# Retention and a two-layer network on one core: q cast without its decay, the decay multiplied into the retention's result, and a new order of the work

## The chip, the cores and the metric

The kernel runs on one core of a Trainium2 chip. The metric is the device time of one execution in microseconds. Three runs of the kernel before gave 282.3, 279.86 and 279.4; their median is 279.86.

The engines are called PE (matmul), DVE (vector), ACT (scalar), POOL and SP. PE's weight loads have a row of their own, PEld. Work that PE writes lands in PSUM; DVE and ACT read it there.

## The reference

q, k and v are f32 of shape 8 x 8 x 576 x 64 (batch, heads, positions, head size). For each batch and head, with gamma = 1 - 2^(-5-head):

```python
scores = scale * np.matmul(q, k.transpose(0, 1, 3, 2))
Dmat = np.where(rel >= 0, gamma[:, None, None] ** rel[None, :, :], 0.0)   # rel = row - column
ret = scores * Dmat
attn = np.matmul(ret, v)
...
x = attn.transpose(0, 2, 1, 3).reshape(B * S, H * D)       # 4608 tokens x 512
h = x @ w_in                                               # 512 x 2048
out = np.maximum(0.01 * h, h) @ w_out                      # 2048 x 512, f32
```

The factor gamma^(row - column) is gamma^row from the side of q times gamma^(-column) from the side of v, so either can be multiplied in on its own.

## The kernel before

**Units and groups.** The tokens are cut into 36 units of 128 tokens; each is two chunks of 64 positions of one batch (a batch has nine chunks). Four units make a group of 512 tokens, nine groups in all. A unit u goes through these jobs, by the names that the order's table uses:

- `ld{u}.1`, `.0`, `.2`: load k, q and v (256 KB each, f32) into one of four tiles each. SP issues k and q from unit 12 on and for unit 0, POOL the rest, the weights and most stores (line 346; w_in is line 612, in four quarters `wi0` to `wi3` of 512 KB as f16).
- `ck`, `cq`, `cv`: to f16. k is only cast (line 371). q is multiplied by scale * gamma^row and v by gamma^(-row): on DVE in one product with a broadcast table (line 375), on ACT in eight narrow multiplies, one for each head (line 381). Rows are counted within a block of 256 positions, and `place(c)` says in which quarter of the block a chunk c lies.
- `tp` and `yt`, for units 0 to 7: q and k are turned by PE (line 411) and copied out of PSUM (line 418). From unit 8 on `tr` turns them by a transposing DMA that SP issues.
- `sa` (scores, line 445) and `sb` (what each chunk adds to the state, line 454): 64x64 matmuls into the PSUM tile `sc`. From unit 4 on `sa` is part of `ca`. `mk` masks the scores from PSUM on DVE (line 460).
- `st`: the running state in f32 on DVE (lines 485 to 491); the one at a block's end goes through a scratch tile `stmp` and is scaled by gamma^256. `sx` casts it to f16.
- `oa`, or `ow` and `ca` from unit 4 on: outputs, 64x64 matmuls into the PSUM tile `ot` (line 542). `ot` has two slots; unit u writes slot u % 2, so `ca{u+2}` waits for the copy of unit u.
- `x{u}`: copies the unit's output from PSUM into the f16 tile xT of its group (line 591), on ACT for 31 units and on DVE for 5.

**The network.** Groups 0 and 1 go through w_in plainly (jobs `h` on PE, line 640, and `l` on ACT, line 647). From group 2 on layer 1 (`a`, line 833), and for all groups layer 2 (`b`, line 911), is done in seven products for eight with sums of operands made on DVE (`xs`, `m`, `ws`, `wm`), seeds copied from PSUM to PSUM (`cA`), and partial results copied out (`u2`, `k5`).

**What sets the order.** The code declares jobs with what they must come after. A long string, ORDER, names all of them in the sequence in which they are issued; each engine runs its own in that sequence. A word such as `tp1.0@0` gives the accumulator bank, and `+13@3` puts 13 matmuls on idle data in (the filler, line 980). The table ENGINE says which of DVE and ACT runs a copy or cast.

Of the kernel before, what the change touches and what calls it, by code (L numbers as in the profile page):

```python
# [33 lines left out]
class Plan:  # L34
# [52 lines left out]
    for eng, names in {  # L87
        "DVE": """
            ck0 cq0 sx0.0 yt0.0 cq1 sx0.1 cv1 cq2 sx1.0 yt2.1 ck3 cq3 yt3.1 cv3 sx2.1 yt3.0 cq4 cv4 x3 ck5 cq5
            cv5 yt5.1 cq6 sx5 cv6 cq7 ck7 cv7 yt7.0 b0.cA cv8 ck10 sx8.0 cv9 cq9 cq11 cq12 cv10 b1.cA cv13 ck15  # L90
            cv14 cq14 cv15 cq15 sx13.1 sx14 cq16 cv16 cv17 cq17 cq18 a2.3.k5 sx17.0 cv18 sx18 cq19 a3.1.u2 x17
            cv20 ck21 cq21 sx19 a3.2.k5 cq22 cv22 sx20 ck23 cv23 cq23 x20 cv24 cq25 sx23 a4.2.cA cv25 a4.2.u2
            cq26 cq27 cv27 sx25 a5.0.u2 a5.0.k5 cq28 cq29 cv29 ck30 cq30 cv30 ck31 cv31 cq32 sx30 cq33 ck33
            a6.0.cA cv33 cv34 ck34 cq35 cq34 a6.2.cA b5.u2 cv35 a6.3.u2 x32 a7.0.cA x33 a7.0.k5 b5.21 a7.1.cA
            b6.11 b6.u2 a7.3.cA a7.3.u2 a8.0.k5 b7.k5 a8.2.u2 a8.2.k5 b7.21 a8.3.u2 b8.21
        """,
        "ACT": """
            cv0 yt0.1 x0 ck1 ck2 yt1.1 yt1.0 cv2 yt2.0 x1 sx1.1 sx2.0 x2 sx3.0 ck4 sx3.1 yt4.1 yt4.0 ck6 sx4.1
            x4 yt5.0 x5 yt6.0 yt6.1 sx6 yt7.1 sx7 x7 x6 ck8 b0.11 cq8 ck9 b0.u2 cq10 b0.k5 cv11 ck12 sx9 x8 ck11
            cv12 sx10 cq13 b0.21 x9 ck13 sx11 b1.11 sx12 x10 b1.u2 x11 ck14 a2.0.cA b1.k5 a2.0.u2 a2.0.k5 x12  # L100
            a2.1.cA a2.1.u2 x13 a2.1.k5 ck16 ck17 sx15 a2.2.cA a2.2.u2 b1.21 a2.2.k5 sx16 x14 a2.3.cA x15
            a2.3.u2 ck18 b2.cA a3.0.cA b2.11 a3.0.u2 a3.0.k5 a3.1.cA cv19 b2.u2 x16 a3.1.k5 ck19 b2.k5 a3.2.cA
            ck20 cq20 a3.2.u2 cv21 b2.21 ck22 x18 a3.3.cA a3.3.u2 a3.3.k5 x19 b3.cA a4.0.cA b3.11 sx21 ck24
            a4.0.u2 a4.0.k5 cq24 a4.1.cA a4.1.u2 sx22.1 a4.1.k5 x21 b3.u2 ck25 b3.k5 ck26 sx24 a4.2.k5 x22 cv26
            a4.3.cA x23 a4.3.u2 a4.3.k5 ck27 b3.21 a5.0.cA b4.cA ck28 cv28 sx26.0 b4.11 x24 ck29 a5.1.cA a5.1.u2
            a5.1.k5 x25 sx27 sx28 b4.u2 a5.2.cA x26 sx29 b4.k5 a5.2.u2 a5.2.k5 x27 a5.3.cA ck32 a5.3.u2 cv32
            a5.3.k5 cq31 b4.21 x28 x29 sx31.1 a6.0.u2 a6.0.k5 sx32 b5.cA a6.1.cA b5.11 a6.1.u2 x30 a6.1.k5 x31
            a6.2.u2 a6.2.k5 sx33 b5.k5 ck35 a6.3.cA a6.3.k5 sx34 sx35.0 a7.0.u2 b6.cA a7.1.u2 a7.1.k5 a7.2.cA
            a7.2.u2 b6.k5 a7.2.k5 x34 x35 a7.3.k5 a8.0.cA b6.21 a8.0.u2 b7.cA b7.11 a8.1.cA b7.u2 a8.1.k5
            a8.1.u2 a8.2.cA a8.3.cA a8.3.k5 b8.cA b8.u2 b8.k5 b8.11x so8.11x b8.11y  # L110
# [26 lines left out]
    ld15.1 m1.0.1 ow10 b0.11 ca11 m1.2.0 a2.0.p1.0@2 b1.11 so0.0 b1.p5.0@0 m1.1.1 a2.0.cA@1 cv13 x10 b1.p5.1 mk11
    sx12 ld17.2 b1.p6.1 m1.2.1 m1.3.0 ow11 b1.u2 sb13 ca12 m1.3.1 a2.0.p2.0 x11 b1.p7.0 tr13 ld15.0 a2.0.11 xs2.0
    cq14 b1.k5 ld16.0 a2.0.p5.0@2 st13.1 b1.p7.1 a2.0.k5 xs2.1 ld17.0 mk12 a2.0.p6.0 xs2.2 b1.p3.0 a2.0.u2 sx13.1
    ck15 ck14 ld16.1 xs2.3 a2.0.p7.0 a2.0.p3.0 a2.0.22 b1.p3.1 a2.0.12 l2.0.22 a2.0.p4.0 b1.22 l2.0.12 a2.1.p1.0@2  # L140
    cv14 a2.0.21 b1.p4.0 b1.12 ld18.2 a2.1.p5.0@1 cq15 sb14 a2.1.k5 ow12 ca13 tr14 a2.1.cA@0 b1.p4.1 st14.0 x12
# [910 lines left out]
```

## Time and profile before

| | us |
|---|---|
| runs | 279.4, 279.86, 282.3 |
| the profiled execution's own time | 279.54 |
| its span in the profile | 277.7 |
| PE busy | 268.1 |
| PE weight loads busy | 224.4 |
| DVE busy | 229.8 |
| ACT busy | 206.7 |
| POOL busy | 72.4 |
| DMA, mean rate over the span | 180 GB/s |

The profile is one execution, taken by the hardware profiler; its span is shorter than the execution's time, since the span ends with the last instruction that the profile shows. Matmuls are pipelined, so a busy PE is one with a matmul under way, and the mean duration of one (273 ns for 128x256) is longer than the step from one to the next (0.87 us for eight, 109 ns each, in the chain of work that ended last). That chain is PE for 91% of the span and DMA for 5%. In a group's row stand line, engine, operation, tiles, shapes and count, then busy time and mean ns of one, then the engine's idle time just before and what ended it.

### The profile page before, as it was taken

How to read it: one execution, taken by the hardware profiler on the slowest of the kernel's cores; microseconds unless marked ns; L12 is line 12 of the kernel's file. 1: busy time of each engine (PE TensorE's matmuls, PEld its weight loads, DVE VectorE, ACT ScalarE, POOL GpSimd, SP SyncE). 2: the span in 40 equal slices, each digit the busy share in tenths (PEclk: the TensorE clock that was granted, in tenths of full speed). 3: DMA queues.
4: the chain of work that ended last, by engine and by line, in shares of the span. 5: the costliest groups of instructions: out<-in, count | busy, mean ns of one | idle time of the engine just before them, and what ended most of it. 6: DMA issues, size and time to landing. Idle time of an engine off the chain costs nothing.

```text
span 277.7 us, 10117 instructions
## 1 busy us (share of the span) xinstructions
PE 268.1 (97%) x4337; PEld 224.4 (81%) x4337; DVE 229.8 (83%) x431; ACT 206.7 (74%) x459; POOL 72.4 (26%) x92
## 2 busy tenths in 40 slices
PE   6878999999999999999999999999999999999994
PEld 2545688888888888888888888888888888888884
DVE  2767767989998999899999999898989885955761
ACT  3846678769977998999889998899765756665630
POOL 8959696401211313222113321120011000200200
PEclk9999999999999999999999999999999999999999
DMA  7999999997899999799999998799041100300123
GB/s 219 224 240 238 293 287 269 277 216 177 208 256 220 220 295 227 173 236 230 257 222 255 183 228 183 170 247 219 20 139 74 44 2 2 153 0 0 78 97 132
DMA packets 94364, 50.04 MB, mean 180 GB/s; under 512 B 83312, under 2 KB 88560, under 8 KB 94320
## 3 DMA queue, kind: packets, MB, share of 16 engines
q1 hardware_dynamic: 82624, 21.37, 40.4%
q0 software_dynamic: 11264, 27.79, 36.1%
q8 instruction: 34, 0.56, 0.8%
q10 hardware_dynamic: 432, 0.24, 0.3%
q14 instruction: 10, 0.08, 0.1%
HBM read 36.81 MB, written 9.44 MB: 167 GB/s over the span
## 4 chain that ended last, share of the span: by engine, by line
PE 91%; DMA 5%; POOL 1%; ACT 1%; issue 1%; DVE 1%; POOLq 0%
PE acc L911 39%; PE acc L833 32%; PE acc L640 10%; DMA t<-in_k_dram 5%; PE ot L542 5%; PE sc L454 2%; PE sc L445 2%; PE sc L911 1%; POOL t L346 1%; PE acc L411 1%; DVE s L487 0%; POOL w_in L612 0%; ACT st L503 0%; DVE qk L375 0%; DVE s L460 0%
## 5 line engine op out<-in xcount | busy, mean ns | idle before, releaser
L911 PEld LDWEIGHTS <-gt 128*128 128x128 f16 x720 | 69.8, 98 | 8.4
L346 POOL DMA_DIRECT2D t<-in_v_dram x40 | 34.2, 857 | 100.5 <-DVE v L375 64.0
L911 PE MATMUL acc<-w_out,gt 128*128 128x256 f16 x416 | 51.5, 273 | 0.0
L833 PEld LDWEIGHTS <-w_in 128*128 128x128 f16 x448 | 42.4, 98 | 5.6
L853 ACT ACTIVATE gt<-acc 128x512 f16<-128x512 f32 x56 | 33.4, 599 | 16.6 <-PE acc L833 16.4
L861 ACT ACTIVATE gt<-sum 128x512 f16<-128x512 f32 x56 | 34.8, 633 | 4.7 <-DVE sum L857 4.7
L911 PE MATMUL acc<-w_mix,gt 128*128 128x256 f16 x288 | 36.2, 273 | 0.0
L833 PEld LDWEIGHTS <-w_sum 128*128 128x128 f16 x336 | 32.2, 98 | 4.1
L833 PE MATMUL acc<-xs,w_sum 128*128 128x256 f16 x224 | 33.6, 273 | 0.0
L833 PE MATMUL acc<-xT,w_in 128*128 128x256 f16 x224 | 33.5, 273 | 0.0
L833 PE MATMUL acc<-xs,w_in 128*128 128x256 f16 x224 | 33.4, 273 | 0.0
L730 POOL DMA_DIRECT2D out_dram<-osb x16 | 11.5, 718 | 83.9 <-ACT acc L772 38.5
L640 PE MATMUL acc<-xT,w_in 128*128 128x256 f16 (+2 forms) x272 | 30.8, 266 | 0.7 <-ACT qkT L418 0.4
L911 PEld LDWEIGHTS <-mix 128*128 128x128 f16 x288 | 28.1, 98 | 3.3
L460 DVE TENSOR_TENSOR s<-sc,cs 128x512 f16<-128x512 f32 x36 | 24.6, 684 | 4.4 <-PE sc L445 2.3
L640 PEld LDWEIGHTS <-w_in 128*128 128x128 f16 x272 | 22.0, 98 | 5.8 <-issue 0.9
L857 DVE TENSOR_TENSOR sum<-acc,k 128x512 f32<-128x512 f32 x28 | 19.2, 686 | 7.9 <-PE acc L833 5.7
L647 ACT ACTIVATE gt<-acc 128x512 f16<-128x512 f32 x32 | 18.2, 601 | 6.3 <-PE acc L640 6.2
L786 ACT COPY k<-acc 128x512 f32<-128x512 f32 x29 | 17.0, 588 | 7.5 <-PE acc L833 3.7
L375 DVE TENSOR_TENSOR qk<-t,cs 128x512 f16<-128x512 f32 x30 | 20.5, 684 | 2.3 <-DMA t<-in_q_dram 2.3
L591 ACT CAST xT<-ot 128x512 f16<-128x512 f32 x31 | 18.2, 588 | 4.6 <-PE ot L542 4.6
L381 ACT ACTIVATE v<-t,cs 128x64 f16<-128x64 f32 x72 | 18.3, 343 | 4.1 <-DMA t<-in_v_dram 3.4
(69 smaller groups left out, 469.7 us busy)
## 6 DMA issues: line engine op xcount, KB each, us to landing
t<-in_v_dram POOLq DMA_DIRECT2D x32, 256.0 KB, 5.1
out_dram<-osb POOLq DMA_DIRECT2D x16, 512.0 KB, 4.5
t<-in_k_dram SPq DMA_DIRECT2D x22, 256.0 KB, 4.8
t<-in_q_dram SPq DMA_DIRECT2D x22, 256.0 KB, 5.0
t<-in_q_dram POOLq DMA_DIRECT2D x10, 256.0 KB, 8.5
t<-in_k_dram POOLq DMA_DIRECT2D x10, 256.0 KB, 6.5
w_in<-in_moe_w_in_dram POOLq DMA_DIRECT2D x4, 512.0 KB, 7.8
w_out<-in_moe_w_out_dram POOLq DMA_DIRECT2D x4, 512.0 KB, 9.7
```

Source lines behind the costliest of these rows:

```text
L346: engine[eng].dma_start(out=t[CH * j : CH * j + rows], in_=(q, k, v)[x][b, :, CH * w : CH * w + rows, :].rearrange("h t d -> t h d"),)
L375: engine[e].tensor_tensor(out=view[0](out), in0=view[1](t32[u, 2 * x][:]), in1=view[1](decay(u, x)), op=MUL)
L381: nc.scalar.mul(out=out[:, at(h), :], in_=t32[u, 2 * x][:, h, :], mul=tab_sb[:, w, x, h : h + 1])
L460: landed[u] = nc.vector.tensor_tensor(out=s[:], in0=sc[:, :, 0], in1=mask_sb.unsqueeze(1).unsqueeze(1).to_broadcast([P, 2, NP, CH]), op=MUL,)
L591: moved[u] = copies[xe](out=x_of(u).rearrange("q c (j t) -> q j c t", j=2), in_=at)
L640: nc.tensor.matmul(out=a[:, n, :], lhsT=w_in16[:, c, (f0 + n) * P : (f0 + n + 1) * P], rhs=x[:, c, t0 : t0 + nt], start=(n == 0 and c == 0 ...
L647: nc.scalar.activation(out=y[:, f0 : f0 + nf, t0 : t0 + nt], in_=a[:], func=mybir.ActivationFunctionType.Lrelu)
L833: nc.tensor.matmul(out=r[:, f, :], lhsT=w[:, c, (2 * n + f) * P : (2 * n + f + 1) * P], rhs=rhs[:, c, :], start=fresh and c == 0 and f == ...
L853: w = op(what, "ACT", lambda: nc.scalar.activation(out=to(), in_=r[:], func=lr), after, [y], [r])
L857: what, "DVE", lambda: nc.vector.tensor_tensor(out=s[:], in0=r[:], in1=plus[:], op=ADD),
L861: f"l{g}.{n}.{what}", "ACT", lambda: nc.scalar.activation(out=to(), in_=s[:], func=lr), [j], [y],
L911: nc.tensor.matmul(out=(r[tb] if isinstance(r, tuple) else r)[:, tb, :], lhsT=lhs[n]()[:, f, tb * P : (tb + 1) * P], rhs=rhs[n][:, f, :], ...
```

## The change

It has these parts.

1. `cq` only casts q, as `ck` casts k (one function, `plain`, line 402 of the changed kernel). The factor scale * gamma^row of q's row is multiplied in where x leaves PSUM: `x{u}` becomes a product of the PSUM tile with a table `q_tab` (line 618), always on DVE. Both are linear in the row of q, so the result is the same up to rounding.
2. `q_tab` (128 x 4 x 4 x 64, f32) is made by four products `tb0` to `tb3` on DVE (line 381) from two small factors that come with the constants; x of a unit waits for the quarters of the table that it uses.
3. The scaled state is added and multiplied in place; `stmp` is gone. f32 states have a pool of their own with three buffers instead of four.
4. The tile `idle` is gone: fillers read a part of w_mix, which is cleared first. A tile `pad` of 192 bytes is put in. By the tiles' sizes w_in and w_out now begin at a multiple of 512 bytes within a partition.
5. ENGINE and ORDER are new throughout, with the same jobs, the four table products and the same seven lots of fillers (33 matmuls).

Cut to the core (the reshaped table of loads says the same in new lines):

```diff
 CFG = dict(
     ld=4,
     ap=4,
+    fp=3,
...
-    tab = np.zeros((P, len(kinds), 2, H))
+    tab = np.zeros((P, len(kinds), H))
...
-        tab[:, w, 0] = gamma[None, :] ** r * scale
-        tab[:, w, 1] = gamma[None, :] ** (-r)
+        tab[:, w] = gamma[None, :] ** (-r)
+    NB, FINE = BLK // CH, 16
+    fine, coarse = np.zeros((P, NP, FINE)), np.zeros((P, NP, BLK // FINE))
+    for c in range(NP):
+        for oo in range(2):
+            rows = slice(CH * oo, CH * oo + CH)
+            fine[rows, c] = gamma[2 * c + oo] ** np.arange(FINE)
+            coarse[rows, c] = gamma[2 * c + oo] ** (FINE * np.arange(BLK // FINE) - BLK / 2) * scale
...
+    q_tab = const_pool.tile([P, NB, NP, CH], FP, name="q_tab")
     ident = const_pool.tile([P, P], F16, name="ident")
+
+    pad = const_pool.tile([P, 48], FP, name="pad")
+    warm = pad[:, 0:1]
...
-    idle = const_pool.tile([P, TOK], F16, name="idle")
-    warm = const_pool.tile([P, 1], FP, name="warm")
+    idle = w_mix[:, 2, 0:2].rearrange("p f n -> p (f n)")
...
+    def q_table():
+        for a in range(NB):
+            def run(a=a):
+                nb = CH // FINE
+                nc.vector.tensor_tensor(
+                    out=q_tab[:, a].rearrange("p c (b r) -> p c b r", b=nb),
+                    in0=fine_sb.unsqueeze(2).to_broadcast([P, NP, nb, FINE]),
+                    in1=coarse_sb[:, :, a].unsqueeze(3).to_broadcast([P, NP, nb, FINE]), op=MUL,
+                )
+
+            steep.append(add(f"tb{a}", "DVE", run))
...
+        def plain(x, e):
+            copies[e](out=by_half(t[:, x]), in_=in_halves(t32[u, x][:]))
...
+        cast[u, 0] = add(f"cq{u}", qe, lambda: plain(0, qe), [loaded[u, 0]], [t], [t32[u, 0]])
...
-                    tmp = t_pool.tile([P, NP, CH], FP, name="stmp")
-                    nc.vector.tensor_tensor(out=tmp, in0=x, in1=before[0][:, before[1]], op=ADD)
+                    nc.vector.tensor_tensor(out=to, in0=x, in1=before[0][:, before[1]], op=ADD)
                     nc.vector.tensor_tensor(
-                        out=to, in0=tmp, in1=gblk_sb.unsqueeze(2).to_broadcast([P, NP, CH]), op=MUL
+                        out=to, in0=to, in1=gblk_sb.unsqueeze(2).to_broadcast([P, NP, CH]), op=MUL
...
     def outer_copy(u, j):
-        xe = by(f"x{u}", "ACT")
+        p0, p1 = place(2 * u), place(2 * u + 1)
...
-            moved[u] = copies[xe](out=x_of(u).rearrange("q c (j t) -> q j c t", j=2), in_=at)
+            moved[u] = nc.vector.tensor_tensor(
+                out=x_of(u).rearrange("q c (j t) -> q j c t", j=2), in0=at, in1=by_place, op=MUL
+            )
...
 ORDER = """
-    ld0.1 ld0.2 ld0.0 ld1.0 ld1.1 ld2.1 ck0 ld2.0 cq0 ld1.2 cv0 cq1 ld2.2 +13@3 tp1.0@0 wi1 tp0.0@1 tp0.1@2 sb0 +4@3
+    tb2 ld0.1 ld0.2 ld0.0 cv0 ck0 ld1.0 ld1.1 ld2.1 ld2.0 ld1.2 ld2.2 cq0 tb0 +13@1 cq1 wi1 tp0.1@0 +4@2 tp0.0@1 ld3.1 sb0 st0.0 ld3.0 yt0.1 yt0.0 ck1 +3@3 ld4.1 tp1.0@1 sa0 sx0.0 yt1.0 tp1.1@3 mk0 ck2 st0.1 cv1
...
```

**The first places, on PE.** Where layer 1 begins, around the turning of q and k of unit 3 (qk_448 before, qk_413 now; ident is the unit matrix, idle and w_mix are the fillers). Before:

```order
L542 MATMUL ot<-qkT,st_366 64x64
...
L980 MATMUL acc<-idle 128x512
...
L411 MATMUL acc<-ident,qk_448 128x128
...
L640 MATMUL acc<-xT,w_in_122 128x256
...
L980 MATMUL acc<-idle 128x512
...
L411 MATMUL acc<-ident,qk_448 128x128
...
L640 MATMUL acc<-xT,w_in_122 128x256
```

Now:

```order
L564 MATMUL ot<-qkT,st_355 64x64
...
L669 MATMUL acc<-xT,w_in_124 128x256
...
L1009 MATMUL acc<-w_mix 128x512
...
L434 MATMUL acc<-ident,qk_413 128x128
...
L564 MATMUL ot<-s_473,v_321 64x64
...
L468 MATMUL sc<-qkT 64x64
```

The first product of layer 1 has moved ahead of the first turning of unit 3, and the second has moved behind the output of unit 2 and beyond the last row shown; the two turnings, of k and of q, stand together. Over the whole program PE's 64x64 matmuls stand in 49 unbroken runs before and in 44 now.

**The second place, on DVE**, its first work in the program (t_1 is a loaded k, t_0 a q, t_2 a v; s is a state or a masked score, xT the unit's x). Before:

```order
L371 CAST qk_147<-t_1_135 128x2x4x64
L375 TENSOR_TENSOR qk_147<-t_0_139,cs 128x2x4x64
L375 TENSOR_TENSOR qk_163<-t_0_141,cs 128x2x4x64
L485 COPY s_222<-sc 128x256
L418 COPY qkT<-acc 128x512
L375 TENSOR_TENSOR qk_228<-t_0_149,cs 128x2x4x64
L375 TENSOR_TENSOR v_258<-t_2_152,cs 128x512
```

Now:

```order
L381 TENSOR_TENSOR q_tab<-cs 128x256
L406 TENSOR_TENSOR v_142<-t_2_138,cs 128x512
L381 TENSOR_TENSOR q_tab<-cs 128x256
L402 CAST qk_174<-t_0_146 128x2x4x64
L508 COPY s_210<-sc 128x256
L402 CAST qk_174<-t_1_148 128x2x4x64
L528 CAST st_246<-s_210 128x256
L441 COPY qkT<-acc 128x512
```

k and q of unit 0 have gone to ACT, v of unit 0 has come from there, and two quarters of the table stand among the first rows.

**The third place, on DVE**, where x of group 2 is complete and its sums `xs` begin. Before:

```order
L813 TENSOR_TENSOR xs<-xT 128x512
L375 TENSOR_TENSOR qk_2017<-t_0_1802,cs 128x2x4x64
L485 COPY s_2028<-sc 128x256
L813 TENSOR_TENSOR xs<-xT,xs 128x512
L460 TENSOR_TENSOR s_2043<-sc,cs 128x512
```

Now:

```order
L618 TENSOR_TENSOR xT<-ot,q_tab 128x2x4x64
L744 TENSOR_TENSOR w_sum<-w_in_124,w_sum 128x2x512
L618 TENSOR_TENSOR xT<-ot,q_tab 128x2x4x64
L842 TENSOR_TENSOR xs<-xT 128x512
L402 CAST qk_1973<-t_0_1832 128x2x4x64
L842 TENSOR_TENSOR xs<-xT,xs 128x512
```

x, which ACT copied, now stands on DVE in line with the sums that read it, and where a scaled q stood there is a cast.

More of the change, by code (lines that the diff above doesn't have):

```diff
@@ L88 @@
         "DVE": """
[L89 to L93, printed above, removed]
@@ L96 @@
+            cq27 cv27 cv28 cv29 cq29 sx27 sx28 cv30 ck30 ck31 cv31 cq31 sx29 cq33 cv35 a6.0.k5 cv33 sx31.1 a6.2.u2
+            cv34 a6.3.k5 a7.0.cA b5.21 a7.0.u2 ck35 sx34 b6.11 a7.3.u2 a8.1.cA a8.2.u2 a8.3.k5 b7.21 b8.k5 b8.21
         """,
         "ACT": """
-            cv0 yt0.1 x0 ck1 ck2 yt1.1 yt1.0 cv2 yt2.0 x1 sx1.1 sx2.0 x2 sx3.0 ck4 sx3.1 yt4.1 yt4.0 ck6 sx4.1
-            x4 yt5.0 x5 yt6.0 yt6.1 sx6 yt7.1 sx7 x7 x6 ck8 b0.11 cq8 ck9 b0.u2 cq10 b0.k5 cv11 ck12 sx9 x8 ck11
-            cv12 sx10 cq13 b0.21 x9 ck13 sx11 b1.11 sx12 x10 b1.u2 x11 ck14 a2.0.cA b1.k5 a2.0.u2 a2.0.k5 x12
@@ L101 @@
[L101 to L110, printed above, removed]
+            ck0 cq0 yt0.1 yt0.0 ck2 cq2 yt1.1 yt2.0 yt2.1 cv2 sx1.0 sx1.1 cq3 yt3.1 ck4 sx2.1 cq4 yt4.1 sx3.0 cq5
@@ L137 @@
[L137 to L141, printed above, removed]
@@ new lines @@
+    st10.0 tr9 st10.1s ck12 b0.p3.0 b0.p7.0 b0.p7.1 b0.22 b0.p3.1 b1.p1.0@1 wm3.1 sb11 ow8 ca9 mk9 sx10 st11.0
+    ld13.1 b0.12 b0.p4.0 cv12 ld15.2 b0.p4.1 b0.p2.1 x8 cq12 ck13 st11.1 h1.6.256@2 b0.11 l1.6.256 m1.0.0 b1.p1.1
+    b1.p5.0@0 ld13.0 tr10 tr11 m1.1.0 m1.0.1 ow9 ld16.2 m1.2.0 b0.21 ca10 b1.cA@3 sb12 so0.1 b1.p6.0 sx11 b1.p5.1
+    st12.0 b1.p2.0 b1.p2.1 m1.3.0 x9 mk10 st12.1s ow10 tr12 ld14.0 ld14.1 cv13 m1.1.1 cq13 ca11 a2.0.p1.0@2 m1.2.1
+    b1.p6.1 mk11 x10 ld15.1 b1.k5 so0.0 ld17.2 tr13 sx12 sb13 ow11 b1.11 ws4.0 ca12 ld15.0 ld16.0 x11 xs2.0 b1.p3.0
@@ L368, in casts, with cv @@
         ke, qe, ve = by(f"ck{u}", "ACT"), by(f"cq{u}", "DVE"), by(f"cv{u}", "DVE")
-        def ck():
-            copies[ke](out=by_half(t[:, 1]), in_=in_halves(t32[u, 1][:]))
-        def scaled(out, x, e, at, view):
-            if e != "ACT":
-                engine[e].tensor_tensor(
-                    out=view[0](out), in0=view[1](t32[u, 2 * x][:]), in1=view[1](decay(u, x)), op=MUL
-                )
+        def plain(x, e):
+            copies[e](out=by_half(t[:, x]), in_=in_halves(t32[u, x][:]))
+        def cv():
+            if ve != "ACT":
+                engine[ve].tensor_tensor(out=s[:], in0=t32[u, 2][:], in1=decay(u), op=MUL)
                 return
@@ L380, in scaled @@
             for h in range(H):
-                nc.scalar.mul(out=out[:, at(h), :], in_=t32[u, 2 * x][:, h, :], mul=tab_sb[:, w, x, h : h + 1])
-        def cq():
-            scaled(t[:, 0], 0, qe, lambda h: 2 * (h % NP) + h // NP, (by_half, in_halves))
-        def cv():
-            scaled(s[:], 1, ve, lambda h: h, (lambda a: a, lambda a: a))
-        cast[u, 1] = add(f"ck{u}", ke, ck, [loaded[u, 1]], [t], [t32[u, 1]])
-        cast[u, 0] = add(f"cq{u}", qe, cq, [loaded[u, 0]], [t], [t32[u, 0]])
+                nc.scalar.mul(out=s[:, h, :], in_=t32[u, 2][:, h, :], mul=tab_sb[:, w, h : h + 1])
+        cast[u, 1] = add(f"ck{u}", ke, lambda: plain(1, ke), [loaded[u, 1]], [t], [t32[u, 1]])
+        cast[u, 0] = add(f"cq{u}", qe, lambda: plain(0, qe), [loaded[u, 0]], [t], [t32[u, 0]])
         cast[u, 2] = add(f"cv{u}", ve, cv, [loaded[u, 2]], [s], [t32[u, 2]])
@@ L586, in outer_copy @@
     def outer_copy(u, j):
-        xe = by(f"x{u}", "ACT")
+        p0, p1 = place(2 * u), place(2 * u + 1)
         def cp():
             at = ot[:, :: -1 if u % 2 else 1, u % 2]
-            moved[u] = copies[xe](out=x_of(u).rearrange("q c (j t) -> q j c t", j=2), in_=at)
-        copied[u] = add(f"x{u}", xe, cp, [j], [xT[u // 4]], [ot_banks])
+            by_place = (
+                q_tab[:, p0 : p0 + 1].to_broadcast([P, 2, NP, CH]) if p0 == p1
+                else q_tab[:, p0 : p1 + 1 : p1 - p0] if p0 < p1
+                else q_tab[:, p0 : (p1 - 1 if p1 else None) : p1 - p0]
+            )
+            moved[u] = nc.vector.tensor_tensor(
+                out=x_of(u).rearrange("q c (j t) -> q j c t", j=2), in0=at, in1=by_place, op=MUL
+            )
+        copied[u] = add(f"x{u}", "DVE", cp, [j] + [steep[p] for p in sorted({p0, p1})], [xT[u // 4]], [ot_banks])
     def outer(u):
```

215 lines of the change are left out of this document (118 added, 97 removed), and 12 rows, old and new, of the table loads.

## The prediction

> **What bounds the kernel now.** I read the page's first two lines of totals first, then the span cut by hand into stages, then the start in order of time.
>
> ```profile
> span 277.7 us, 10117 instructions
> PE 268.1 (97%) x4337; PEld 224.4 (81%) x4337; DVE 229.8 (83%) x431; ACT 206.7 (74%) x459; POOL 72.4 (26%) x92
> ```
>
> ```profile
> 1.20:16.60 15.40, 13.04 (x207) 6.40 (x207) 7.74 (x17) 10.02 (x27) 12.48 (x15) 1.00 0.97 253
> 16.60:25.30 8.70, 6.37 (x151) 4.80 (x151) 7.15 (x15) 4.12 (x9) 7.50 (x10) 1.00 1.00 227
> 25.30:60.00 34.70, 34.55 (x559) 27.26 (x560) 27.56 (x54) 24.89 (x53) 21.06 (x25) 1.00 1.11 266
> 60.00:140.00 80.00, 80.00 (x1499) 68.90 (x1497) 75.54 (x146) 71.68 (x172) 16.40 (x20) 1.00 1.05 228
> 140.00:180.00 40.00, 40.00 (x701) 34.41 (x700) 38.23 (x74) 36.37 (x82) 9.05 (x11) 1.00 0.94 205
> 180.00:274.20 94.20, 94.15 (x1229) 82.65 (x1226) 73.22 (x128) 59.24 (x121) 5.74 (x8) 1.00 0.32 86
> 274.20:277.70 3.50, 0.00 (x0) 0.00 (x0) 0.00 (x0) 0.36 (x1) 0.00 (x0) 0.92 0.32 112
> ```
>
> In the stage rows (the second fence) the second number is the stage's length, then busy time of PE, its weight loads, DVE, ACT and POOL, then the granted clock, the DMA share and GB/s. From 25.30 to 274.20 PE is busy 248.70 of 248.90 us at a granted clock of 1.00. Nothing that DVE or ACT saves there can shorten the program: it would only lengthen their idle time. What can move the end is (a) the time before 25.30, where PE has gaps and runs filler matmuls on idle data, (b) how PE's own matmuls follow each other, and (c) a new wait inside the full stretch. The last 3.50 us are one copy and a store, and the profiled execution's own time, 279.54 us, is 1.84 above its span.
>
> The start in order of time, where the bound is the arrival of q, k, v and w_in:
>
> ```profile
> 16.04 0.60 PE L980 MATMUL acc<-idle 128*128 128x512 f16 x2
> 16.16 0.59 ACT L591 CAST xT<-ot 128x512 f16<-128x512 f32 x1 [1.05 <-PE ot L542]
> 17.23 0.68 DVE L371 CAST qk<-t 128x512 f16<-128x512 f32 x1 [2.23 <-DMA t<-in_k_dram]
> 17.97 0.40 PE L411 MATMUL acc<-ident,qk 128*128 128x128 f16 x4 [1.33 <-DVE qk L371]
> 18.20 1.04 PE L640 MATMUL acc<-xT,w_in 128*128 128x256 f16 x8
> 19.08 0.59 PE L980 MATMUL acc<-idle 128*128 128x512 f16 x2
> 19.09 0.68 DVE L375 TENSOR_TENSOR qk<-t,cs 128x512 f16<-128x512 f32 x1
> 19.09 0.62 ACT L371 CAST qk<-t 128x512 f16<-128x512 f32 x1 [2.34 <-DMA t<-in_k_dram]
> 19.82 0.40 PE L411 MATMUL acc<-ident,qk 128*128 128x128 f16 x4 [0.15 <-DVE qk L375]
> 20.06 1.04 PE L640 MATMUL acc<-xT,w_in 128*128 128x256 f16 x8
> ```
>
> The reader is to see that DVE sat idle 2.23 us until k of unit 3 landed at 17.23, and that PE sat idle 1.33 us behind it. In that time only fillers were ahead of the transposition of k.
>
> **The change, part by part.** The rows that price it (line, engine, operation, count, then busy us and mean ns of one):
>
> ```profile
> L375 DVE TENSOR_TENSOR qk<-t,cs 128x512 f16<-128x512 f32 x30 | 20.5, 684 | 2.3 <-DMA t<-in_q_dram 2.3
> L381 ACT ACTIVATE qk<-t,cs 128x64 f16<-128x64 f32 x48 | 12.2, 345 | 0.0
> L381 ACT ACTIVATE v<-t,cs 128x64 f16<-128x64 f32 x72 | 18.3, 343 | 4.1 <-DMA t<-in_v_dram 3.4 <-PE ot L542 0.6
> L371 ACT CAST qk<-t 128x512 f16<-128x512 f32 x24 | 14.8, 622 | 2.3 <-DMA t<-in_k_dram 2.3
> L371 DVE CAST qk<-t 128x512 f16<-128x512 f32 x12 | 5.5, 466 | 5.0 <-DMA t<-in_k_dram 5.0
> L591 ACT CAST xT<-ot 128x512 f16<-128x512 f32 x31 | 18.2, 588 | 4.6 <-PE ot L542 4.6
> L591 DVE CAST xT<-ot 128x512 f16<-128x512 f32 x5 | 3.4, 685 | 0.5 <-PE ot L542 0.5
> L460 DVE TENSOR_TENSOR s<-sc,cs 128x512 f16<-128x512 f32 x36 | 24.6, 684 | 4.4 <-PE sc L445 2.3 <-PE sc L454 2.0
> L487 DVE TENSOR_TENSOR s<-sc,s 128x256 f32<-128x256 f32 x40 | 16.7, 418 | 3.0 <-PE sc L454 2.3 <-PE sc L445 0.5
> ```
>
> *DVE.* It loses the 30 scaled q (20.5 us) and the 5 plain copies of x (3.4). It gets 13 more plain casts of q and k (13 x 0.466 = 6.1). All 36 x become a product of a PSUM tile with a table, which no row shows; the nearest is the masking on L460, the same shapes from PSUM times a table in SBUF: 36 x 0.684 = 24.6. Bounds: below, the plain DVE copy of the same tile, 0.685, in effect the same; above, that copy and L375's scaling as two instructions, 1.369, which would fill DVE and hand the case to the first rival. I take the masking, whose shapes are the same. The four table products are 128x256 as on L487: 4 x 0.418 = 1.7. Of the other work, 10 copies from PSUM go to ACT (-10 x 0.685 = -6.9) and 4 copies of a transposed tile (nearest 0.418: -1.7). Three scaled v come (+3 x 0.684 = 2.1), and 5 casts of states (nearest 0.466: +2.3). Together -20.5 - 3.4 + 6.1 + 24.6 + 1.7 - 6.9 - 1.7 + 2.1 + 2.3 = +4.3 us, so DVE stands at about 234.
>
> *ACT.* It loses 48 narrow multiplies of q (12.2), 24 of the 72 of v (24/72 x 18.3 = 6.1), 31 x (18.2) and 5 state casts (3.1). It gets 23 casts (23 x 0.622 = 14.3) and 14 copies from PSUM (14 x 0.588 = 8.2). Together -17.1, about 190.
>
> Both sums cost or bring nothing by themselves, because PE's full stretch hides them: DVE is idle 80.00 - 75.54 + 40.00 - 38.23 = 6.23 us between 60 and 180, where it is fullest, and 120/274 of its 4.3 extra, some 1.9, fits. Should that cover go, each microsecond that DVE is late is one of PE's; that is the first rival. The scaled state, now added and multiplied in place instead of through a scratch tile, is the same two instructions of the same size: nothing. Three buffers of f32 states for four: their last readers are the next unit's sum and the cast of the state, both on the same in-order engines long before the third unit after: nothing on the path, at worst one DVE instruction of 0.42 at a few units.
>
> *PE, the order.* The matmuls are the same 4337, the fillers the same 33. What the order changes is how often a run of 64x64 matmuls (scores, states, outputs) stands between matmuls of the full array. Such a change of kind costs, as here:
>
> ```profile
> 124.95 0.60 PE L833 MATMUL acc<-xs,w_in 128*128 128x256 f16 x4
> 125.48 0.32 PE L542 MATMUL ot<-s,v 64*64 64x64 f16 x16
> ...
> 125.98 0.61 PE L833 MATMUL acc<-xs,w_in 128*128 128x256 f16 x4
> 126.43 0.60 PE L833 MATMUL acc<-xT,w_sum 128*128 128x256 f16 x4
> 126.87 1.91 PE L911 MATMUL acc<-w_out,gt 128*128 128x256 f16 x16
> ```
>
> Four products take 126.87 - 126.43 = 0.44 us when the next is of their kind, 125.48 - 124.95 = 0.53 ahead of small ones, and 0.45 just behind them: 0.10 for each run of small ones. The order has 49 such runs before and 44 now: 5 x 0.10 = -0.5 us. Bounds: 0 if the five were inside waits of the start, -0.5 if all were in the full stretch.
>
> *The start.* The first product of layer 1 (8 matmuls, 1.04 us on the 18.20 row) now stands ahead of the transposition of k of unit 3. It needs x of units 0 and 1, ready at 16.16 + 0.59 = 16.75, and a quarter of w_in, which had landed by 18.20 at the latest. Placed at about 17 it fills the 1.33 us gap: -1.04. But the second product of layer 1 and the output of unit 2 now stand behind the transposition of q of unit 3, which waits for its cast. q's cast goes to ACT (0.62) and can start no later than 19.09, when the next load of the same ring, k of unit 4, was already there; so that transposition can be as late as 19.8 and PE may sit idle from 18.8, up to 1.0. The row of 19.09 shows DVE taking q without a wait, so q was there earlier and I take 0.6 of this loss: together -0.4. The moved x, now on DVE, is behind a scaled v there at unit 2. Bounds: at best all PE gaps from 16.60 to 25.30 (8.70 - 6.37 = 2.33) and the two pairs of fillers in and ahead of them (0.60 + 0.59) close, -3.5; at worst two DVE instructions of 0.68 stand newly ahead of what PE waits for, +1.4. The four table products lie in DVE's idle time before v of unit 0 and between later loads (DVE is busy 7.74 of 15.40 us there): nothing; without that cover, 1.7.
>
> *The aligned loads.* q, k and v began at a multiple of 512 bytes before too (75776); it is w_in and w_out that move, from 17376 and 33760 to 22016 and 38400 (the built programs' addresses). Their rate beside that of the others:
>
> ```profile
> 20.60:22.20 1.60, 1.50 (x73) 1.13 (x71) 1.36 (x4) 0.24 (x1) 1.60 (x3) 1.00 1.16 181
> 33.00:37.00 4.00, 4.00 (x79) 3.49 (x66) 2.35 (x4) 3.50 (x7) 3.75 (x5) 1.00 1.03 338
> ```
>
> The first stretch is w_in, 181 GB/s written as f16, so 362 GB/s read as f32; the second is q, k and v, 338 read and written, already aligned. Source bytes run at the same rate in both, so the write's place is not what paces the weights: 0. Bounds: 0, and, if writes set the pace and could run at the 338 of the others, a quarter of w_in (512 KB) in 1.5 us in place of 2.8: -1.3. [...]
>
> **Sum.** 279.54 - 0.5 - 0.4 + 0 = 278.6 us. The profiled execution lies 0.32 under the median of the runs shown (279.86; 279.4 to 282.3), so this is 1.2 under that median. About 1% (2.8 us) is what a measurement of this kernel can tell from no change.
>
> **Rivals.**
> *x late on DVE: slower.* x of unit u frees the PSUM half that the scores and outputs of unit u+2 write. It came from ACT, idle 120 - 71.68 - 36.37 = 11.95 us between 60 and 180; now it queues in order on an engine with 6.2, less 1.9. In the new order I count 8 of 30 units where under 1.2 us of PE work stands between x and that use (5 before). If one more DVE instruction is ahead each time, PE waits 8 x 0.684 = 5.5: 278.6 + 5.5 = 284.1. It decides from about six such waits. For it: DVE's 95% in that stretch. Against it: in the same stretch DVE was as full before and PE never waited.
> *The whole start closes: faster.* -3.5 in place of -0.4: 275.5; two thirds of it, 276.6, is already over 1%. For it: k and q of unit 0 and 1 are cast on two engines at once and v of unit 0 in one DVE instruction, 0.68 for 8/72 x 18.3 = 2.0. Against it: k of unit 3 still lands at 17.23, and w_in behind it.
> *The weights land sooner because they are aligned:* -1.3, 277.3. For it: k of unit 3 and w_in share one ring. Against it: the two rates above.
> *The change of order does not do what it says:* the five runs and the moved product cancel against new gaps: 279.5, which the measurement cannot tell from the forecast.
>
> **How the numbers follow.** Forecast with the last rival 0.60, aligned weights 0.06, whole start 0.17, late x 0.17. Faster by over 1% is the whole start: 0.17. Slower by over 1% is late x: 0.17. The rest, 0.66, is within 1%. Low end 276.4, just under two thirds of the start; high end 282.8, where half of late x with the worst start ends (278.6 + 2.8 + 1.4).
>
> **What would show it.** Right: PE without a gap from about 25 us to the last 3.5 us of the span; span near 276.8; DVE near 234 and ACT near 190; x at 36 instructions near 0.69 each; the first layer-1 product at about 17 us, and k of unit 3 still cast at about 17.2. Wrong: PE waits named after x or its table product between 60 and 200 us (late x); a full PE from 21 or 22 us on (whole start); the cast of k of unit 3 at 16.5 or sooner (aligned weights).

## The result and the profile after

The changed kernel takes 289.31 us (median of 6 runs, 287.7 to 292.15) against 279.69 for the kernel before beside it (6 runs, 279.12 to 282.3). The ratio is 1.0316, 95% interval 1.027 to 1.0361: slower by about 9 us, where 278.6 was forecast and 282.8 was the upper end. Medians and ranges in this document are of all runs of a kernel; the ratios leave out runs over 1.5% above the fastest of the same kernel, and they compare with runs of the kernel before made beside them. The profiled execution took 288.94 us, with a span of 287.2.

The page's totals of the changed kernel:

```profile
span 287.2 us, 10042 instructions
PE 271.1 (94%) x4337; PEld 226.6 (79%) x4337; DVE 232.3 (81%) x443; ACT 192.1 (67%) x388; POOL 72.7 (25%) x92
```

DVE and ACT are close to where they were forecast. PE has 3 us more of busy time for the same 4337 matmuls and stands at 94% for 97%: it waits, and part of its work ran slower. The same stages as before, with the same columns (start, length, busy time of PE, its weight loads, DVE, ACT, POOL, then granted clock, DMA share, GB/s):

```profile
1.20:16.60 15.40, 13.85 (x211) 7.26 (x212) 10.21 (x22) 9.29 (x21) 12.86 (x16) 1.00 1.02 266
16.60:25.30 8.70, 7.53 (x167) 5.83 (x166) 6.23 (x13) 5.99 (x13) 7.95 (x11) 1.00 1.03 224
25.30:60.00 34.70, 29.77 (x523) 22.89 (x521) 26.73 (x51) 23.61 (x45) 20.18 (x24) 1.00 1.15 251
60.00:140.00 80.00, 76.34 (x1324) 65.18 (x1324) 68.83 (x134) 56.17 (x120) 15.57 (x19) 0.96 1.00 217
140.00:180.00 40.00, 40.00 (x753) 34.47 (x751) 39.62 (x80) 31.22 (x65) 8.42 (x10) 1.00 1.01 216
180.00:274.20 94.20, 94.20 (x1285) 82.73 (x1282) 75.52 (x138) 63.98 (x123) 7.51 (x10) 1.00 0.35 83
```

The loss is in two rows. From 25.30 to 140 PE is idle 4.93 + 3.66 = 8.6 us, where it had been idle 0.15, and the clock between 60 and 140 is 0.96. The start is better than before: PE is busy 13.85 + 7.53 = 21.38 us up to 25.30, for 19.41. PE's waits between 26 and 284 us name what it waited for (total us, times, longest):

```profile
PE ot L564 <- DMA qkT<-qk: 6.5, 1, 6.5
PE sc L477 <- issue: 1.3, 1, 1.3
PE sc L468 <- issue: 0.4, 1, 0.4
PE acc L669 <- DMA w_in<-in_moe_w_in_dram: 0.2, 1, 0.2
```

No wait of this stretch is named after x. One wait makes up most of the loss: the cross products of unit 8 (`ca8` in the order) wait 6.5 us for a transposing DMA, the first that the kernel uses (units 0 to 7 are turned by PE). PE at that place, in order of time:

```profile
55.44 0.32 PE L477 MATMUL sc<-v,qk 64*64 64x64 f16 x16
62.25 0.32 PE L564 MATMUL ot<-qkT,st 64*64 64x64 f16 x6 [6.50 <-DMA qkT<-qk]
...
62.73 1.89 PE L940 MATMUL acc<-w_mix,mix 128*128 128x256 f16 x8
64.41 1.92 PE L940 MATMUL acc<-w_out,gt 128*128 128x256 f16 x8
```

Eight of these products took 1.04 us in the kernel before; here they take 1.9. The stage rows around the place show why (clock in the third column from the end):

```profile
50.00:60.00 10.00, 5.76 (x67) 4.93 (x65) 7.45 (x14) 5.57 (x12) 0.97 (x2) 1.00 1.20 214
60.00:67.00 7.00, 4.75 (x45) 3.45 (x45) 5.81 (x11) 0.51 (x1) 0.88 (x1) 0.52 0.99 186
67.00:70.00 3.00, 3.00 (x29) 2.69 (x28) 0.50 (x2) 0.59 (x1) 0.00 (x0) 0.99 1.10 204
```

The wait begins at 55.75; from 60.21, 4.5 us into it, to 67.04 the granted clock is 0.50 (0.52 in the row for the 7 us from 60), which is 3.4 us of lost work, and in the row from 67 it is back at 0.99. Shorter waits, told below, came with less: one of 2.5 us (`ca8` used later) and one of 2.2 us (unit 8 turned by PE) lie in stages with a clock of 0.98 and 0.96, some 1.6 us of lost work each. One of 1.7 us (unit 8 turned by PE, earlier) lies in a stage with 1.00. How long a wait must be to cost clock is not shown.

Now SP's queue in both kernels (start, time to issue), the changed one first:

```profile
47.95 1.58 SPq L420 DMA_TRANSPOSE qkT<-qk  x1
49.71 0.44 SPq L363 DMA_DIRECT2D t<-in_k_dram  x1
50.26 7.59 SPq L363 DMA_DIRECT2D t<-in_q_dram  x1
57.95 5.50 SPq L420 DMA_TRANSPOSE qkT<-qk  x1
```

```profile
56.36 1.33 SPq L397 DMA_TRANSPOSE qkT<-qk  x1
57.87 0.44 SPq L346 DMA_DIRECT2D t<-in_k_dram  x1
58.42 0.52 SPq L346 DMA_DIRECT2D t<-in_q_dram  x1
```

The change issues the transposition 8.4 us earlier: q of unit 8 is now one cast on ACT that stands earlier and ends at 47.92, where eight narrow multiplies ended at 56.34. But it lands only at 62.2: 14.3 us after its issue, where it took 3.6 before (and landed at 60.0). What else used the DMA engines from the issue to the landing (packets, MB, share of 16 engines; q1 carries SP's transfers, q0 POOL's), in the changed kernel and in the one before:

```profile
q0 software_dynamic: 1430, 2.44, 82.4%
q1 hardware_dynamic: 1769, 0.44, 34.8%
```

```profile
q1 hardware_dynamic: 1706, 0.43, 69.0%
q0 software_dynamic: 86, 0.25, 21.3%
```

The same 0.44 MB of SP's went through in both windows, in 14.4 us beside 2.44 MB of POOL's (w_out and later q, k, v), and in 3.7 us beside 0.25 MB. In the first 4 us, from 48 to 52, the view has a row for POOL's queue and none for SP's:

```profile
q0 software_dynamic: 680, 1.04, 116.0%
```

So the theory T1: the new order brings the cross products of unit 8 forward by about 6 us (PE is ready for them at about 55.6, for 61.7). The transposition that they read is 8.4 us earlier, so it would be early enough at its old 3.6 us; but it now falls into the time when POOL's queue streams the weights, where it takes four times as long. PE runs dry and its clock halves. The sum: 8.4 us of named waits + 3.4 of clock - 2.0 in the start - 0.5 for five fewer runs of small matmuls = 9.3, for a span that is 9.5 longer. The rivals are R1 (x late on DVE), the layout, and R2 (the stretch is bound by the transfers whatever PE does).

### The profile page after: what moved, and what is told of

It is laid out like the page before. It is cut to its first block, busy times and chain, and to the rows that moved or that the text cites. A ratio compares the mean times of both kernels' runs of the same rounds, so it can differ in the third digit from the quotient of the medians.

```text
span 287.2 us, 10042 instructions
## 1 busy us (share of the span) xinstructions
PE 271.1 (94%) x4337; PEld 226.6 (79%) x4337; DVE 232.3 (81%) x443; ACT 192.1 (67%) x388; POOL 72.7 (25%) x92
## 4 chain that ended last, share of the span: by engine, by line
PE 81%; DMA 10%; issue 2%; DVE 2%; POOL 1%; ACT 1%; SPq 1%
PE acc L940 35%; PE acc L862 29%; PE acc L669 6%; DMA qkT<-qk 5%; PE ot L564 4%; DMA w_in<-in_moe_w_in_dram 3%; PE acc L1009 2%; DMA t<-in_k_dram 2%; PE sc L477 2%; PE sc L468 2%; PE sc L940 1%; POOL t L363 1%; SPq L363 1%; PE acc L434 1%; DVE s L483 0%
## 5 line engine op out<-in xcount | busy, mean ns | idle before, releaser
L940 PE MATMUL acc<-w_out,gt 128*128 128x256 f16 x416 | 52.4, 275 | 0.0
L882 ACT ACTIVATE gt<-acc 128x512 f16<-128x512 f32 x56 | 33.4, 598 | 15.8 <-PE acc L862 15.3
L402 ACT CAST qk<-t 128x512 f16<-128x512 f32 x47 | 28.3, 620 | 9.4 <-DMA t<-in_q_dram 4.4
L862 PE MATMUL acc<-xs,w_in 128*128 128x256 f16 x224 | 32.7, 273 | 0.0
L815 ACT COPY k<-acc 128x512 f32<-128x512 f32 x32 | 18.6, 587 | 15.3 <-PE acc L940 10.7
L618 DVE TENSOR_TENSOR xT<-ot,q_tab 128x512 f16<-128x512 f32 x36 | 24.6, 684 | 1.9 <-PE ot L564 1.8
L801 ACT COPY acc<-acc 128x512 f32<-128x512 f32 x33 | 19.1, 578 | 8.9 <-PE acc L862 6.5
L812 ACT COPY u<-acc 128x512 f32<-128x512 f32 x31 | 18.2, 588 | 9.9 <-PE acc L862 5.9
```

The costliest lines, as they stand in the source:

```text
L402: copies[e](out=by_half(t[:, x]), in_=in_halves(t32[u, x][:]))
L618: moved[u] = nc.vector.tensor_tensor(out=x_of(u).rearrange("q c (j t) -> q j c t", j=2), in0=at, in1=by_place, op=MUL)
L801: copies[ce](out=B[:], in_=A[:])
L815: op("k5", ke, lambda: copies[ke](out=k5[:], in_=C[:]), [done["5"]], [k5], owned(C))
L862: nc.tensor.matmul(out=r[:, f, :], lhsT=w[:, c, (2 * n + f) * P : (2 * n + f + 1) * P], rhs=rhs[:, c, :], start=fresh and c == 0 and f == ...
L882: w = op(what, "ACT", lambda: nc.scalar.activation(out=to(), in_=r[:], func=lr), after, [y], [r])
```

## The experiments

**The two halves of the change apart.** The first kernel has the new arithmetic, layout and buffers in the old order:

```
-ORDER, ENGINE = those of after
+ORDER = "tb0 tb1 tb2 tb3 " + the order of before; ENGINE = that of before
```

> The changed arithmetic (q only cast, its decay in the product that makes x, on DVE), layout and buffers, in the old order with the old assignment of engines; the four table products stand first on DVE. Theory T1 (the new order lets PE reach the cross products of unit 8 at 55.5 us, 6.5 us ahead of the transposition they read, and the clock then halves for 6.8 us): the transposition of unit 8 has four layer-2 products between it and its use again, so no such wait: 278 to 281 us. Rival R1 (x late on DVE, which is now the only engine that makes x): PE waits named after x, 284 to 289 us.

Measured: 286.03 us, ratio 1.0226 (1.0165 to 1.0286). R1's time; T1's range, 278 to 281, is missed. It is also R1's way, in a wider form: no transposing DMA is waited for, the clock is 1.00 in every stage, and PE's waits after 5 us, 7.0 us in all, name DVE many times, most of them small. x itself is named for 1.5 us of them, and nearly all the rest is other work on the same engine. The three longest:

```profile
PE acc L434 <- DVE qk L402: 1.8, 2, 1.4
PE acc L669 <- DVE xT L618: 1.0, 3, 0.3
PE ot L564 <- DVE s L483: 0.9, 2, 0.6
```

In this order the end of PE's n-th matmul falls behind that of the kernel before step by step (0.7 us at the 150th, 1.6 at the 900th, 4.0 at the 1800th, 6.8 at the 3600th). So late DVE work is a real mechanism of this arithmetic in the old order, with about the size that the prediction gave it (6 us for 5.5); in the changed kernel PE's waits after 26 us name no work of DVE. The kernel of this run also has the four table products ahead of all other DVE work, which is part of the first 0.7 us.

The second has the old arithmetic in the new order:

```
-ORDER, ENGINE = those of before
+ORDER = the order of after without tb0 .. tb3; ENGINE = that of after
```

> The arithmetic and layout of the kernel before (q scaled in its cast, x a plain copy, weights not at multiples of 512 bytes), in the new order with the new assignment of engines. T1: the wait at unit 8 and the halved clock are there: 286 to 291 us. R1 and the layout as the cause: 277 to 281 us.

Measured: 307.76 us, ratio 1.0986. The forecast of T1 is missed by 17 us and the run doesn't decide: the new table of engines puts 24 q on ACT, which in the old arithmetic are eight narrow multiplies each, and all 36 x as well. ACT grows to 239 us:

```profile
PE 278.3 (90%) x4337; PEld 228.6 (74%) x4337; DVE 214.7 (69%) x403; ACT 239.3 (77%) x592; POOL 72.2 (23%) x92
```

PE's longest wait there is 4.8 us for x from ACT. So the order of the changed kernel can't be tried with the old arithmetic in this way.

**The wait at unit 8 removed, in two ways.** First, only the place of its use:

```
-tr8 sb10 wm2.1 ld12.1 ca8 cq9 ... mk8 cq11 ... b0.p6.1 b0.k5 b0.u2 ws4.1
+tr8 sb10 wm2.1 ld12.1 cq9 ... cq11 ... b0.p6.1 ca8 b0.k5 b0.u2 mk8 ws4.1
```

> The changed kernel, with the cross products of unit 8 and their masking behind four layer-2 products and a pair of layer-1 products, near where the kernel before has them; nothing else moved. T1: the transposition still lands at 61 to 63 us, 13 to 15 us after its issue, but PE has work until then, short of up to 1.5 us of waiting for the last quarter of w_out (landed at 58.5), and the clock stays full: 279 to 282 us. Rival R2 (the transfers of 45 to 62 us bound that stretch whatever PE does, and it runs dry until 62): 286 to 289 us. R1: 289 us.

Measured: 283.49 us (281.33 to 288.55), ratio 1.0101 (1.0055 to 1.0147). That is 1.5 us above T1's range, but R1 and R2, at 286 us and more, fall. The transposition lands at 62.2 as before, 14.8 us after its issue, and PE has work until then. PE's longest waits:

```profile
PE sc L475 <- issue: 2.5, 1, 2.5
PE acc L938 <- DVE w_out L713: 1.4, 1, 1.4
```

No wait for qkT is left, and the 1.4 us for the last quarter of w_out is the one expected. The four runs at a granted clock of 1.00 took 281.3 to 282.7. The other six had 0.988 to 0.994; in the profiled one of them the clock between 60 and 140 us is 0.98, and eight products take 1.89 us right behind the 2.5 us wait that is named "issue" (it ends at 98.17), for 1.05 ahead of it. That wait is taken up below. This wait and this clock are where T1's range was missed in this profile; the runs without a profile don't show where they lost clock.

Second, without the transposing DMA:

```
-turned=8,
+turned=9,
-... b0.p1.1 b0.cA@3 cq10 h1.2.256@2 ... tr8 sb10
+... tp8.1@2 yt8.1 b0.p1.1 b0.cA@3 cq10 tp8.0@1 yt8.0 h1.2.256@2 ... sb10
```

> The changed kernel with unit 8 turned by PE like units 0 to 7 (8 matmuls and two copies on DVE added, one transposing DMA gone). T1: the cross products of unit 8 find their data at 55.5 us; the next transposing DMA, of unit 9, may land as late as 62 to 65 us, but its use is some 10 us of PE work later: 278 to 281 us. R2: PE runs dry at the next transposition or at the last quarter of w_out, 284 to 289 us. R1: 289 us.

Measured: 282.34 us (280.48 to 286.56), ratio 1.0064 (1.0022 to 1.0105); 1.3 us over the range, and faster than the changed kernel by some 7 us. The profiled run, 285.07 us, has a wait of 2.2 us for ACT and a granted clock of 0.96, both between 140 and 180 us, far from unit 8. The cross products of unit 8 now follow without a gap, at 56.66:

```profile
56.52 0.32 PE L476 MATMUL sc<-v,qk 64*64 64x64 f16 x16
56.66 0.23 PE L563 MATMUL ot<-qkT,st 64*64 64x64 f16 x8
```

**Why the transposition lands late.** SP held until w_out has landed:

```
+hold on SP: nc.sync.dma_start(out=gate[0:1, 0:2], in_=w_out16[0:1, 15, 0:2])
-h1.0.256@1 tr8
+h1.0.256@1 hold tr8
```

> The changed kernel with one 4-byte DMA ahead of the transposition of unit 8 on SP, which reads the last quarter of w_out: SP, and so this transposition and all loads behind it, starts only when that quarter has landed, 8 to 9 us later than in the changed kernel. Theory T1 with its cause, that SP's small packets (256 bytes) get little of the 16 DMA engines while POOL's queue streams large ones: w_out lands by 57.5 in place of 58.5, the transposition is issued at about 57 and lands within 3.5 to 5.5 us, at 60.5 to 62, no later than in the changed kernel although it starts 9 us later; PE still waits 5 to 6.5 us and the clock still halves: 286 to 290 us. Rival Rd (the transposition is slow by itself, or because of what PE, ACT and DVE do then): it needs 10 us or more again, lands at 67 or later: 293 us or more.

Measured: 306.12 us, ratio 1.0893. The total missed by 16 us: w_out landed at 64.8 instead of 57.5 and everything behind SP came later still; this kernel also lost PE work and clock already before 25 us (11.94 + 6.54 us of busy PE up to 25.30, at a clock of 0.92 and 0.94), for a reason that was not found. The point in dispute can be read all the same. The step in the chain of waits, and the queues from 65.6 to 70.9:

```profile
65.67 4.97 DMA qkT<-qk
```

```profile
q1 hardware_dynamic: 2053, 0.52, 70.6%
q0 software_dynamic: 147, 0.43, 42.4%
```

With most of POOL's stream over, the same transposition takes 5.0 us. So it is not slow by itself. PE is idle in all of that time, though (7.28 us up to 70.68), so the other half of Rd, that the engines' work slows it, is not settled here. The opposite test leaves their jobs where they are and holds POOL back:

```
+hold on POOL: nc.gpsimd.tensor_copy(out=pad[:, 1:2], in_=qkT[8][:, 0, 0, 0:1])
-wo3 ld11.1 ... ld13.2 ... ld11.0 ... ld14.2 ... tr8
+wo3 ... tr8 hold ld11.1 ld13.2 ld11.0 ld14.2
```

> The changed kernel with four loads of POOL's queue (k and q of unit 11, v of units 13 and 14; 1 MB of 2.4 MB that it moves between 48 and 62 us) held back, by a one-column copy on POOL that reads the turned unit 8, until that transposition has landed. T1: with some 40% of the competing bytes gone it lands at 55 to 58 us in place of 62.2; PE waits 0 to 2.5 us, the clock stays full: 280 to 284 us, unless the delayed k of unit 11 is then late (its use is 15 us later). Rival Rd: landing at 61 to 63 us, 288 to 290 us.

Measured: 284.62 us, ratio 1.0177 (1.0124 to 1.0231), 0.6 us above T1's range; the profiled run, 284.03, has a mean granted clock of 0.992. The transposition lands at 57.8, after 8.8 us, as T1 has it, and Rd falls (PE waits 0.6 us for it):

```profile
48.98 8.79 DMA qkT<-qk
```

```profile
q0 software_dynamic: 1128, 1.50, 79.8%
q1 hardware_dynamic: 2065, 0.52, 40.6%
```

The four landings go with POOL's bytes in the same time: 0.25 MB, 3.6 us; 0.43, 5.0; 1.50, 8.8; 2.44, 14.3. A straight line through them starts near 2.5 us and rises 4.7 us for each MB. The line describes and doesn't prove, since a longer transfer also lets more of POOL's bytes pass; the evidence is that in the two tests above POOL's part was changed on purpose and the landing followed. How the DMA engines share their time between the two queues is not shown, nor why none of SP's packets pass at first: in the changed kernel SP's first packet comes 4.15 us after the issue (52.10), in the kernel before 1.27 us after it (57.63). What holds it there stays open.

**Whether the half clock comes from PE's idle time.** Matmuls on idle data ahead of the wait, first 18, then 26:

```
-tr8 sb10 wm2.1 ld12.1 ca8 cq9 ... l1.0.256 l1.2.256
+tr8 sb10 wm2.1 ld12.1 cq9 l1.2.256 l1.0.256 +18@1 ca8 ...        (then +26@1)
```

> The changed kernel with 18 matmuls of 128x512 whose result nobody reads ahead of the cross products of unit 8 (5.3 us of PE work), and two copies of layer 1 and a cast ahead of them for a free PSUM bank. T1: the transposition lands at about 62 as before, PE is idle for about 1 to 2 us in all instead of 6.5, so the clock does not halve and 3.4 us come back: 285 to 286.5 us. Rival Rc (the halved clock is not caused by PE's idle time): still 0.5 for some 7 us, 288 to 290 us.

Measured: four runs from 283.49 to 291.07 us. In the profiled one the transposition landed at 64.7, PE still waited 2.8 us, and the mean granted clock is 0.988, as in the changed kernel's profile. That doesn't decide.

> As with 18 fillers ahead of the cross products of unit 8, but 26 of them (7.6 us of PE work). T1: PE has no idle time over 1 us there, and the clock shows no half stretch between 55 and 75 us in the profile: 284.5 to 286.5 us. Rival Rc (the half clock there is not caused by the idle time): a stretch of 3.4 to 6.8 us at half clock stays between 55 and 75 us, 288 to 291 us.

Measured: 285.8 us (285.36 to 288.45), ratio 1.0223 (1.0182 to 1.0265), as T1 has it. The transposition still takes 15.4 us, PE waits 0.9 us for it, and the stage rows are:

```profile
50.00:60.00 10.00, 9.56 (x81) 6.36 (x80) 6.53 (x12) 5.04 (x11) 0.89 (x1) 1.00 1.25 169
60.00:67.00 7.00, 6.11 (x73) 4.88 (x71) 6.29 (x12) 0.54 (x2) 0.88 (x1) 1.00 0.96 208
```

Twenty-six matmuls whose result nobody reads make the program faster, by 3.5 us from median to median (2.6 by the two ratios), because the clock there stays at 1.00. Rc falls.

**The layout alone**, in the kernel before:

```
+pad = const_pool.tile([P, 8], FP, name="pad")        (ahead of w_in16: now at byte 17408)
+tail = const_pool.tile([P, 120], FP, name="tail")    (behind the constants)
```

> The kernel before with only w_in, w_out and the sums of weights moved to multiples of 512 bytes in SBUF by 32 bytes of padding (and 480 behind them, so that q, k and v keep such multiples too). That alignment does not matter: the first quarter of w_in lands as in the kernel before (by about 18 us), 279.4 to 280.7 us. [...]

Measured: 281.01 us, ratio 1.0021 (0.9983 to 1.0058), 0.3 us above the expected range and not faster. k of unit 3 is cast at 17.17, for 17.23: alignment brings nothing that can be seen.

**What is left when unit 8 is mended.** Turned by PE as above, with its two transpositions about 2 us earlier and one copy on ACT:

```
-... l1.14.256 wm2.0 ... tp8.1@2 yt8.1 b0.p1.1 b0.cA@3 cq10 tp8.0@1 yt8.0 h1.2.256@2
+... l1.14.256 tp8.1@2 yt8.1 wm2.0 ... tp8.0@1 yt8.0 b0.p1.1 b0.cA@3 cq10 h1.2.256@2       (yt8.0 on ACT)
```

> As with unit 8 turned by PE, but its two transpositions stand some 2 us of PE work earlier and apart, and one of the two copies is on ACT, so that no layer-1 product waits for them (1.0 us there). T1: 281.0 to 281.7 us less about 1: 279.5 to 281 us; the wait of about 1.2 us in the middle of the state products of unit 15, put down to nothing the profile shows, stays, since it sits at one place of PE's instruction stream (recorded instruction 3264, as 1473 and 6592 are, 256 apart or a multiple), whatever job is there.

Measured: 281.19 us (12 runs), ratio 1.0057 (1.0031 to 1.0084), 0.2 us above the range. The wait for a copied tile is down to nothing, but a wait of 1 us for w_out took its place, and the one in the middle of the state products of unit 15 stayed:

```profile
PE sc L476 <- issue: 1.7, 1, 1.7
PE acc L939 <- DVE w_out L714: 1.0, 1, 1.0
```

In the changed kernel that wait is inside a job of 16 matmuls, behind the 11th; in the kernel with eight more matmuls ahead (unit 8 on PE) it is the same job, behind the 3rd:

```profile
102.85 0.31 PE L477 MATMUL sc<-v,qk 64*64 64x64 f16 x11
104.43 0.23 PE L477 MATMUL sc<-v,qk 64*64 64x64 f16 x5 [1.26 <-issue]
```

```profile
95.00 0.21 PE L476 MATMUL sc<-v,qk 64*64 64x64 f16 x3
96.22 0.29 PE L476 MATMUL sc<-v,qk 64*64 64x64 f16 x13 [1.01 <-issue]
```

Counted over the weight loads and matmuls that start before it, the matmul behind the gap is preceded by 3257 of them in both kernels, and the one behind the shorter wait at 43.65 us by 1465, which is 7 times 256 fewer. (The texts on record count seven or eight more records of PE's queue, hence 3264 and 1473.) PE's weight loads and matmuls, 8674 in all, come to about 34 times 256, and the page of the changed kernel has a queue with as many packets of 16 KB:

```profile
q8 instruction: 34, 0.56, 0.8%
```

So the last experiment moves the stream under the jobs:

```
-+13@1
+nudge@1 +4@1     (nudge: 72 matmuls of 128x64 on idle data)
```

> The same, with 9 of the 13 first fillers (128x512) replaced by 72 matmuls of 128x64, which take the same time but move every later PE instruction 126 places on in the stream. Theory T2 (those waits are PE waiting for its own instructions, fetched 256 at a time in packets of 16 KB over the DMA engines; the block of 256 that ends at 3264 holds two bursts of 64x64 matmuls and is used up in 3.7 us): the wait at the state products of unit 15 goes, since no block is then shorter than 4.9 us: 278 to 279.8 us, 1 to 1.4 below the kernel of the same call without the shift. Rival R3 (a wait for data that the profile does not name): it stays at the same job, same time.

Measured: 281.7 us (median of 12 runs; the profiled run 279.85), ratio 1.0034 (1.0001 to 1.0066). One of the 12 runs took 948.89 us, for a reason that no trace shows. T2's forecast of the time, 278 to 279.8, is missed: in time the kernel can't be told from the one without the shift (1.0031 to 1.0084). In the trace T2's mark is plain, the same job without a gap:

```profile
94.45 0.32 PE L467 MATMUL sc<-qkT 64*64 64x64 f16 x16
94.58 0.35 PE L476 MATMUL sc<-v,qk 64*64 64x64 f16 x16
```

R3 falls. The wait was moved, not removed everywhere: the one of 0.4 us that is still named "issue" here, at 127.9 in another job, stands behind 4537 weight loads and matmuls, which is 3257 and 5 times 256. In all traces together 17 waits of 0.2 us or more carry this name. Thirteen stand at the same remainder of 256, the four between 22 and 28 us two further on. In the changed kernel's trace the two at 44.09 and 104.43 end 1.4 and 1.6 us after one of the packets of 16 KB is through (42.70 and 102.86). The packets and the distance of the waits agree with T2. That PE waits there for its own instructions remains the author's reading of these counts; no row of the profile names it. What stays open is why the time doesn't follow; no version has a ratio under 1.

## Why the prediction was wrong

*The step that failed* is "What the order changes is how often a run of 64x64 matmuls ... stands between matmuls of the full array." It was taken as the whole effect of the order outside the start. The order, with the shorter cast, also changes when a DMA is issued, and so on which side of another queue's stream it falls. The prediction had named the right kind of danger, "a new wait inside the full stretch", and then looked for it at x alone; of `tr8`, which the order moves, no time was worked out. The distance between issue and use alone would have given comfort: 7.6 us in the new kernel, 5.3 in the old. What was missing is what else is in flight at the new time of issue. The kernel before shows it. POOL's queue there from 47.9 to 56.3, when its own transposition began:

```profile
q0 software_dynamic: 1345, 2.26, 114.0%
```

That stream would have had to be passed. An estimate from it, if the transposition gets its share only when the stream is through, is 56.3 + 3.6 = 59.9, some 4.3 us of waiting for PE: a rival on the slow side that the prediction did not have.

*The cost of one wait* would have been mis-sized too: 6.5 us of idle PE cost 3.4 more through the clock. Late x was priced without a clock, rightly, since its waits are short (in the arithmetic in the old order none is over 1.4 us, and the clock stayed at 1.00).

*DVE and ACT:* forecast "about 234" and "about 190", measured 232.3 and 192.1. The row that had to be chosen for x, the masking, was right to the nanosecond:

```profile
L618 DVE TENSOR_TENSOR xT<-ot,q_tab 128x512 f16<-128x512 f32 x36 | 24.6, 684 | 1.9 <-PE ot L564 1.8
```

*"Both sums cost or bring nothing by themselves"* holds for the new order as far as PE's waits show it (none after 26 us names DVE or ACT), and is wrong for the arithmetic in the old order, where it costs 2.3%. *The late-x rival* (284.1) had about the right size for that case, with late DVE work in general rather than x alone, and the wrong order for this one.

*The start* was mis-sized: -0.4 forecast, -2.0 by PE's busy time up to 25.30. The first product of layer 1 starts at 16.19, k of unit 3 is cast at 16.61 (17 and 17.2 were forecast). The loss feared behind q of unit 3 came as priced: its transposition waits 0.53 us for the cast on ACT, and 0.6 was taken. So the gain besides it was about 2.5 us, where the prediction had 1.0. Why k lands 0.6 us sooner was not tried; alignment alone, in the old order, gave 0.06.

*The aligned loads* at 0: shown, for the old order. *The five runs of small matmuls* at -0.5: no run isolates them. PE's busy time grew by 3.0 us where the clock alone would add 3.4; the rest, -0.4, has their sign and about their size.

*The range* ended at 282.8 because it held no case in which a transfer is late.

## What to carry to other kernels

When an order brings a use forward, count two things for each DMA it reads: the work that is left between issue and use, and the bytes that other queues have in flight at the new time of issue; an earlier issue is no earlier landing (62.2 here, for 60.0). Price a long wait of PE with the clock: 6.5 us of idle time cost 3.4 more here, waits of 2.2 and 2.5 us came with some 1.6 more in two runs, one of 1.7 us with none, and 26 cheap filler matmuls brought 3.5 us back. Arithmetic and order that were made for each other could not be judged apart here: this arithmetic cost 2.3% in the old order and 0.6% or less in its own once unit 8 was mended.
